# Attention and an MLP mixer in one kernel: two of six pairs of row tiles of the last batch's first channel product from seven half products, and a new order list

## The chip, the cores and the metric

The kernel runs on one core of one Trainium2 chip. A core has a matrix engine (TensorE, PE in the profile; its weight loads are PEld), three engines for element-wise work (VectorE, DVE; ScalarE, ACT; GpSimd, POOL), and an engine that mostly issues transfers (SyncE, SP). Each engine works through its own instructions in order and waits for others by semaphores. The metric is the device time of one execution in microseconds; the figure of a kernel is the median of its runs.

## The reference

Four batches, eight heads, 768 positions, 64 values a head. Attention sees a window of the last 128 positions and 4 sink positions. Its output, 768 x 512 for each batch, goes through a mixer: a product over positions, and then one over channels with 1536 hidden rows.

```
scores = (q @ k^T) / 8, kept where key < 4 or 0 <= query - key < 128
a = softmax(scores);  x = a @ v            # 768 x 512 for a batch
h = relu(x^T @ w_tok1) @ w_tok2            # over positions, 256 hidden
u = x + h^T
out = u + relu(u @ w_ch1) @ w_ch2          # over channels, 1536 hidden
```

Inputs and output are float32; the products are taken in bfloat16 and summed in float32.

## The kernel before

**Tiling.** Heads are handled in eight groups of four, g = 0 to 7, two groups to a batch. For a group, q and k are loaded, cast to bfloat16 (copies at L436 and L438) and turned; scores are formed at L827, the sink scores at L834, exponentials at L871, masks at L882 to L904 (on DVE or POOL, by the table MASK_ENG), and the weighted sums at L930 to L939. A weighted sum carries its row sum as a 65th column: DVE takes the reciprocal into one of four small tiles `rc` (L956, L963) and multiplies (L957, L969). The sink keys are copied to the tiles `ks` at L436 or L438 (engine by the table KS_ENG).

**Mixer.** The token products are at L1001 (with a ReLU into `h1` at L1060 or L1062) and L1043; L1049 adds to give `u`, and a DMA transpose (L1055) writes it as `uT`: four blocks of 128 channels by 768 positions. The first channel product makes tiles: one tile is 128 hidden rows by one half (384) of the positions, from four matmuls of 128x384 at L1103, and ACT or DVE writes its ReLU into `v1` (L1060, L1062). There are 12 row tiles and two halves, 24 tiles for a batch.

**Seven products, already there.** In the batches 1 to 3 the second channel product is cut into 2 x 2 blocks and formed by seven products of half size in place of eight. Its sums of `v1` are at L1129, its products at L1154, and the additions of its results on DVE at L1182 to L1187; stores are issued at L1240. The four sums of `w_ch2` that it needs are made once (L1078).

**What sets the order.** The program is a list of tasks, numbered as they are created (937 before). A planner in the file walks a simulated clock: whenever an engine is free, it takes the task that is ready and has the lowest number in the list RANK, one entry a task, and it hands a task with several possible engines to the one that would end it first. The order that comes out is the order in which instructions are issued; on the chip each engine keeps to it. PSUM is given out as eight banks: four singles (ps_ga to ps_gd) and two pairs (ps_sa, ps_sb); from a bank's first matmul to the last read of it no other task has it. Tasks that matter below: 340 and 341, a token product of batch 1 and its ReLU; 488, a cast of q for group 4; 23 and 24, the loads of the second half of `w_ch2` and of group 2's k, both on POOL's queue.

The core of a tile of the first channel product and the loop of the last three batches:

```
nc.tensor.matmul(flat(slot)[:, 0:HS], w_ch1[:, c, ts(ft, P)], uT_[:, c, ds(half * HS, HS)],
                 start=(c == 0), stop=(c == NC - 1))
...
for ft in range(NF):
    ch1(0, ft)
for x in range(NH):
    ch1(1, x)
    ch1(1, NH + x)
```

Of the kernel before, what the change touches and what calls it, by code (L numbers as in the profile page):

```python
# [46 lines left out]
MASK_ENG = {0: ('POOL',), 1: ('POOL', 'DVE'), 2: ('POOL',), 3: ('POOL',), 4: ('POOL', 'DVE'), 5: ('DVE',), 6: ('POOL',), 7: ('POOL',)}  # L47
KS_ENG = {0: ('ACT',), 1: ('POOL', 'ACT', 'DVE'), 2: ('POOL',), 3: ('ACT',), 4: ('POOL', 'ACT', 'DVE'), 5: ('ACT', 'DVE'), 6: ('ACT',
    'DVE'), 7: ('ACT', 'DVE')}
# [7 lines left out]
RANK = [-600, 12, 27, 429, 496, 90, 80, 0, 0, 10, 50, 100, 100, 140, 150, 1507, 62, 576, 219, 821, 901, 915, 1175, 1647, 1601, 2145,  # L57
    1923, 2170, 2665, 2875, 3140, 100, 90, 450, 210, 190, 1763, 1381, 1469, 1468, 1260, 1733, 3285, 3322, 95, 299, 389, 145, 379, 442,
    514, 731, 743, 0, 472, 507, 557, 803, 857, 894, 510, 655, 712, 836, 964, 1070, 1232, 1252, 708, 783, 574, 762, 873, 870, 1001, 1017,
    1152, 1164, 1282, 1299, 1479, 1410, 1547, 1640, 1584, 1529, 1604, 1677, 1701, 2119, 2114, 1916, 1972, 2086, 2166, 2132, 2156, 2111,  # L60
    2199, 2312, 981, 1053, 1235, 1303, -3, 1101, 1155, 1389, 1497, 1248, 1303, 1476, 1558, 1681, 1657, 1392, 1497, 1643, 1756, 1510,
    1407, 1712, 1787, 1772, 1907, 2076, 2226, 2127, 2185, 2249, 2279, 2157, 2229, 2895, 2249, 2265, 2388, 2390, 2456, 2480, 2038, 2671,
    2119, 1943, 2361, 2356, 2283, 2369, 1775, 2491, 2498, 2528, 2631, 3263, 3295, 3100, 3150, 2592, 2234, 2656, 3072, 3592, 3121, 3192,
    2924, 2994, 3023, 3093, 2895, 2795, 3170, 3241, 2974, 3424, 3220, 3290, 3789, 3875, 3724, 3810, 3404, 3550, 3334, 3420, 4179, 3745,
    3529, 3615, 3594, 3080, 3399, 3485, 3339, 3355, 4021, 4087, 3891, 4028, 4149, 4205, 4410, 5149, 4214, 4300, 3956, 4044, 4129, 4335,
    4475, 4578, 4570, 4626, 4727, 4946, 4822, 4909, 4662, 4782, 5010, 5118, 5263, 5369, 5348, 5434, 4857, 5055, 5480, 5569, 5964, 5709,
    5956, 6320, 6780, 6554, 6796, 6644, 6454, 6884, 6982, 6989, 7179, 7540, 7720, 7784, 7266, 7735, 7951, 8080, 8334, 8306, 8376, 8956,
    8785, 8850, 3951, 3767, 4045, 3745, 4116, 4144, 4377, 4433, 3857, 3942, 3854, 3912, 4054, 4013, 4314, 4368, 4518, 4605, 4713, 4819,
    5203, 5304, 5330, 5420, 4504, 5240, 5052, 5010, 5437, 5573, 5192, 5224, 5588, 5749, 5674, 5730, 5795, 5851, 5830, 5921, 5865, 6181,
    4850, 5107, 4808, 5770, 4977, 4911, 4963, 4998, 5413, 5480, 5446, 5521, 5586, 5606, 5612, 5695, 5936, 5900, 5989, 6058, 6164, 6205,  # L70
    6352, 6442, 5802, 5915, 6280, 6438, 6550, 6822, 6977, 7035, 6730, 6775, 6783, 6919, 7075, 7153, 7110, 7254, 7144, 7204, 6123, 6129,
    6108, 6265, 7417, 7504, 7352, 7438, 7648, 7734, 7834, 7542, 7794, 7959, 7821, 7908, 8084, 7864, 7967, 8209, 8071, 8142, 8384, 7907,
    8027, 8509, 4368, 4350, 4385, 4647, 4095, 4742, 4760, 4922, 8886, 8372, 8764, 8850, 8951, 9067, 9302, 9432, 9081, 9167, 8976, 9104,
    9277, 9323, 9447, 9469, 9432, 9518, 9926, 9972, 9725, 9811, 9660, 9746, 9790, 9876, 10527, 10613, 10272, 10358, 10267, 10213, 10402,
    10548, 10575, 10661, 10640, 10786, 10705, 10851, 10830, 10916, 11026, 11052, 11166, 11252, 11234, 11320, 10411, 10656, 10718, 10888,
    10840, 10935, 11079, 11220, 11305, 11404, 11485, 11580, 10397, 11119, 10895, 11393, 11487, 11628, 11648, 11654, 11713, 11314, 11472,
    11800, 11844, 11931, 12278, 11874, 10901, 11047, 11091, 11177, 11582, 11669, 12520, 11996, 12172, 12303, 12389, 12437, 11956, 12193,
    12240, 12511, 11305, 11422, 12041, 12127, 12299, 11865, 12237, 12324, 11975, 13099, 12565, 12633, 12371, 12496, 12561, 12707, 5274,
    5339, 5289, 5389, 5439, 6183, 6051, 5916, 6158, 6252, 6263, 6307, 6429, 6511, 6286, 6354, 6462, 6540, 6511, 7241, 6302, 6811, 6611,
    7483, 7561, 7630, 6898, 7067, 7133, 6988, 7000, 7085, 7646, 7573, 7737, 7377, 8059, 8092, 8353, 8402, 8114, 8162, 8184, 8252, 8149,  # L80
    8952, 8218, 8302, 5774, 5489, 5584, 5679, 5869, 6014, 6029, 6194, 7232, 6764, 6686, 7153, 7465, 6852, 7403, 8438, 8718, 8503, 8546,
    8636, 8829, 8907, 8976, 9226, 9246, 9193, 9363, 8653, 8703, 9019, 9107, 9380, 9449, 9075, 9258, 9497, 9542, 9521, 9592, 9556, 9492,
    9625, 9692, 9590, 9742, 8485, 8611, 8590, 8388, 9855, 9941, 9920, 10007, 10051, 10055, 10399, 10034, 10175, 10214, 10532, 10656,
    10684, 10137, 10175, 10619, 10180, 10234, 10809, 10224, 10294, 11329, 12901, 12957, 12564, 12692, 12629, 12715, 12694, 12790, 12816,
    12902, 13011, 13097, 12946, 13032, 13155, 13241, 13220, 13306, 13302, 13388, 13367, 13453, 13490, 13576, 13565, 13641, 13725, 13781,
    14120, 14086, 14065, 14151, 14160, 14246, 14335, 14421, 14583, 14679, 14979, 15065, 14452, 14547, 14914, 15000, 15164, 15250, 15262,
    15348, 14245, 14303, 14499, 14659, 15010, 15180, 15278, 15423, 15376, 15471, 15552, 14964, 14370, 14457, 14517, 14604, 15589, 15676,
    15524, 15592, 15741, 15958, 16045, 16092, 16024, 16152, 16343, 16293, 14648, 14724, 14725, 14817, 15890, 15936, 16176, 16305, 16307,
    16569, 16697, 16763, 16634, 16730, 16777, 16837, 14790, 15777, 15327, 15489, 16241, 16338, 16372, 16379, 16438, 16423, 16590, 16637,
    16700, 16973, 16887, 16711, 9134, 9249, 9324, 9514, 9609, 9799, 9854, 10024, 8397, 9826, 10144, 10623, 11001, 10994, 11219, 12376,  # L90
    12356, 12437, 12520, 12610, 12759, 12987, 12906, 13076, 13267, 12576, 13293, 12627, 12739, 12953, 13111, 13283, 13419, 13285, 13353,
    13432, 13477, 13456, 14127, 13620, 13676, 13655, 13726, 13690, 13776, 9989, 9894, 9419, 10524, 10119, 11064, 11444, 11569, 9641,
    10983, 11442, 12106, 12875, 11664, 12963, 13748, 13728, 13791, 13890, 13980, 13991, 14205, 14326, 14353, 14443, 14533, 13997, 14109,
    14341, 14547, 14707, 14843, 14713, 14767, 14856, 14910, 14880, 14960, 15044, 15100, 15079, 15178, 15119, 15446, 13955, 14021, 13879,
    13956, 15413, 15479, 15458, 15545, 15655, 15719, 15793, 15615, 15979, 16048, 15578, 15659, 15798, 15806, 15871, 16043, 16089, 16185,
    16433, 16132, 16245, 16518, 16765, 16851, 16895, 16981, 17871, 17957, 17155, 17241, 17025, 16811, 16830, 16916, 16960, 16986, 17030,
    17116, 17160, 17246, 17525, 17371, 17350, 17436, 18015, 17501, 17480, 17566, 18001, 18087, 17545, 17631, 17741, 17827, 17806, 17892,
    18262, 18348, 17936, 18022, 18197, 18283, 18327, 18413, 18392, 18478, 18522, 18608, 18457, 18543, 17685, 18141, 18221, 18302, 18076,
    18431, 18493, 18555, 18662, 18709, 18790, 18871, 18066, 18188, 17610, 18269, 18915, 19018, 18784, 18319, 19111, 18733, 18637, 19078,
    18926, 19132, 19180, 19272, 18132, 18350, 17676, 18397, 18980, 19067, 18849, 18952, 19177, 18718, 18838, 19413, 19439, 19526, 18973,  # L100
    19337, 18587, 18985, 19242, 19329, 19308, 19454, 19433, 19520, 19504, 19387, 19493, 20170, 19656, 19715, 17196, 19591, 19675, 19635,
    19690, 19765, 19669, 19723, 19757]
STRASSEN = {1, 2, 3}
EARLY_P = {1: 0, 2: 0, 3: 4}
TURNS = '10 20 11 21 60 50 61 40 70 51 41 30 12 71 22 62 52 31 72 32 42'
S_CHUNK = 2
S_ENG = {1: ('DVE',), 2: ('DVE',), 3: ('DVE',)}
T_ENG = ('POOL', 'DVE')

SEM = 0.05  # L110
PE_TAIL = 0.16


# [211 lines left out]
def dve(n):  # L325
    return n * 0.00104 + 0.065
# [11 lines left out]
def kernel(  # L338
# [13 lines left out]
    nc = tc.nc  # L352
# [436 lines left out]
    def make_scores(g):  # L789
# [84 lines left out]
        for j in range(2):  # L874
# [11 lines left out]
            def m1(t, dst=dst, lo=1, hi=NT):  # L886
# [11 lines left out]
                for i in range(2):  # L898
# [14 lines left out]
                    [G.exp[j, 1], G.exp[j, 2], t_mask1], prio=pr(g, "mk", j), port=True)  # L913
            G.ready[j, 0], G.ready[j, 1], G.ready[j, 2] = [a], [c], [d]

    rcs = [0]

    def make_pv(g):
        G, s, b = Gs[g], g % 2, g // GB
# [484 lines left out]
```

## Time and profile before

| | us |
|---|---|
| median of 10 runs | 200.41 (200.16 to 201.94) |
| profiled execution, its time | 201.38 |
| span of the profiled execution | 199.7 |
| PE busy | 193.3 |
| DVE busy | 135.4 |
| ACT busy | 108.7 |
| POOL busy | 77.0 |

The span runs from the first to the last instruction; 1.7 us of the execution lie around it. A row of the profile gives an engine, a line of the kernel, the operation, the tile written and the tiles read, and times in microseconds. A busy PE is not PE at its peak, since matmuls overlap their neighbours: how far apart neighbouring matmuls start says more. In a timeline, the brackets at the end of a row give the engine's idle time before it and what ended it.

### The profile page before, as it was taken

The page shows a single profiled execution, that of the slowest core. Times are in us where ns is not written, and L with a number is a line of the kernel's source. Part 1 is how long each engine was busy: PE and PEld are TensorE (multiplying, and loading weights), DVE is VectorE, ACT ScalarE, POOL GpSimd, SP SyncE. Part 2 cuts the span into 40 slices and gives each one's busy share as a digit, 9 for nine tenths or more (in the row PEclk, how much of TensorE's full clock was granted, in tenths as well). Part 3 has the DMA queues.
Part 4 walks back from the last instruction along what each step waited for, and adds up shares of the span by engine and source line. Part 5 has one row for each costly group of instructions (what it writes and reads, how often), then busy time and mean ns, then how long its engine had stood idle before and what let it go on. Part 6 is the DMA issues. An engine that isn't in the chain of part 4 may idle for free.

```text
span 199.7 us, 4626 instructions
## 1 busy us (share of the span) xinstructions
PE 193.3 (97%) x1799; PEld 130.0 (65%) x1799; DVE 135.4 (68%) x312; ACT 108.7 (54%) x191; POOL 77.0 (39%) x132
## 2 busy tenths in 40 slices
PE   7999999999998999999999999999999999999993
PEld 2544876656675565666756687567677787666882
DVE  4688872479758489757578865475799974146883
ACT  2799478889897833289425202867824003764100
POOL 8994432125999663200632020992970000000000
PEclk9999999999999999999999999999999999999999
DMA  5999999999399999899997998350000168000053
GB/s 171 363 225 181 208 279 271 225 268 192 101 281 181 249 169 129 226 127 240 214 171 131 185 196 184 113 128 0 0 3 0 32 171 257 21 0 0 0 187 132
DMA packets 75016, 31.00 MB, mean 155 GB/s; under 512 B 63667, under 2 KB 71475, under 8 KB 74995
## 3 DMA queue, kind: packets, MB, share of 16 engines
q0 software_dynamic: 29680, 10.22, 41.9%
q1 hardware_dynamic: 44082, 18.85, 41.6%
q10 hardware_dynamic: 1232, 1.64, 2.3%
q8 instruction: 14, 0.23, 0.5%
q14 instruction: 8, 0.06, 0.1%
HBM read 26.77 MB, written 6.29 MB: 166 GB/s over the span
## 4 chain that ended last, share of the span: by engine, by line
PE 74%; DMA 15%; DVE 4%; SPq 2%; POOL 2%; issue 1%; ACT 0%; ACTq 0%; DVEq 0%; POOLq 0%
DMA w_tok<-in_moe_w_tok_dram 8%; PE ps_gd L1103 8%; PE ps_ga L1103 7%; PE ps_gb L1103 7%; PE ps_gc L1103 7%; PE ps_gd L1154 5%; PE ps_gc L1154 4%; PE ps_gb L1154 4%; DMA q32b<-in_q_dram 4%; DMA k32a<-in_k_dram 3%; PE ps_ga L1154 3%; SPq L481 2%; PE ps_sa L1154 2%; PE ps_sa L827 2%; PE ps_ga L1262 1%; PE ps_gd L1262 1%
## 5 line engine op out<-in xcount | busy, mean ns | idle before, releaser
L1103 PEld LDWEIGHTS <-w_ch 128*128 128x128 bf16 x384 | 36.5, 98 | 22.9 <-issue 0.8
L1154 PEld LDWEIGHTS <-v 128*128 128x128 bf16 x222 | 21.0, 98 | 4.3 <-issue 0.9
L1060 ACT ACTIVATE v<-ps_ga 128x384 bf16<-128x384 f32 x22 | 10.8, 491 | 15.9 <-PE ps_ga L1103 14.9
L1060 ACT ACTIVATE v<-ps_gb 128x384 bf16<-128x384 f32 x20 | 9.8, 492 | 11.5 <-PE ps_gb L1103 11.0
L1060 ACT ACTIVATE v<-ps_gd 128x384 bf16<-128x384 f32 x15 | 7.4, 491 | 9.3 <-PE ps_gd L1103 9.2
L1103 PE MATMUL ps_gb<-uTb,w_ch 128*128 128x384 bf16 x56 | 11.4, 326 | 0.0
L481 POOL DMA_DIRECT2D vab<-in_v_dram x4 | 5.7, 1437 | 14.0 <-PE ps_gd L939 11.4
L1060 ACT ACTIVATE v<-ps_gc 128x384 bf16<-128x384 f32 x18 | 8.8, 491 | 4.0 <-PE ps_gc L1103 3.6
L1103 PE MATMUL ps_gd<-uTa,w_ch 128*128 128x384 bf16 x52 | 10.6, 326 | 0.0
L1262 PEld LDWEIGHTS <-v 128*128 128x128 bf16 x72 | 6.3, 98 | 6.3 <-issue 1.0
L1001 PEld LDWEIGHTS <-w_tok 128*128 128x128 bf16 x96 | 9.1, 98 | 1.9 <-issue 0.4
L1103 PE MATMUL ps_gc<-uTa,w_ch 128*128 128x384 bf16 x48 | 9.8, 326 | 0.0
L1103 PE MATMUL ps_ga<-uTa,w_ch 128*128 128x384 bf16 x48 | 9.8, 326 | 0.0
L1103 PE MATMUL ps_gc<-uTb,w_ch 128*128 128x384 bf16 x44 | 9.0, 326 | 0.0
L1103 PE MATMUL ps_ga<-uTb,w_ch 128*128 128x384 bf16 x44 | 8.9, 326 | 0.0
L481 POOL DMA_DIRECT2D vaa<-in_v_dram x4 | 5.9, 1478 | 7.3 <-PE ps_gb L939 6.0
L1129 DVE TENSOR_TENSOR x_bb<-v 128x768 bf16<-128x768 bf16 x6 | 3.7, 615 | 7.2 <-ACT v L1060 7.2
L1103 PE MATMUL ps_gd<-uTb,w_ch 128*128 128x384 bf16 x40 | 8.1, 326 | 0.0
L882 POOL TENSOR_TENSOR pTa<-pTa,mask 128x512 bf16<-128x512 bf16 x2 | 2.3, 1153 | 13.7 <-ACT pTa L871 13.7
L871 ACT ACTIVATE pTc<-ps_sb 128x1024 bf16<-128x1024 f32 (+1 forms) x6 | 5.8, 959 | 3.3 <-PE ps_sb L827 3.3
L1103 PE MATMUL ps_gb<-uTa,w_ch 128*128 128x384 bf16 x36 | 7.3, 326 | 0.0
L871 ACT ACTIVATE pTb<-ps_sa 128x1024 bf16<-128x1024 f32 (+1 forms) x7 | 7.0, 997 | 0.5 <-PE ps_sa L827 0.5
(429 smaller groups left out, 555.0 us busy)
## 6 DMA issues: line engine op xcount, KB each, us to landing
q32a<-in_q_dram SPq DMA_DIRECT2D x4, 384.0 KB, 5.5
vaa<-in_v_dram POOLq DMA_DIRECT2D x4, 384.0 KB, 11.2
vab<-in_v_dram POOLq DMA_DIRECT2D x4, 384.0 KB, 12.0
w_ch<-in_moe_w_ch_dram POOLq DMA_DIRECT2D x3, 512.0 KB, 14.9
w_ch<-in_moe_w_ch_dram POOLq DMA_DIRECT2D x2, 768.0 KB, 20.1
q32b<-in_q_dram SPq DMA_DIRECT2D x8, 192.0 KB, 4.5
k32b<-in_k_dram SPq DMA_DIRECT2D x8, 192.0 KB, 6.5
out_dram<-oa SPq DMA_DIRECT2D x4, 256.0 KB, 6.6
```

The source lines that it names most:

```text
L481: t = add(eng, hold, lambda t: e.dma_start(out=o, in_=i), deps, prio=prio, dma=work, run=run)
L827: nc.tensor.matmul(half(slot, i)[:, at:at + w].rearrange("p (c q) -> p c q", q=P), qkT(kT, g, j)[ds(64 * i, 64), kt], qkT(qT, g, j)[ds(64 ...
L871: nc.scalar.activation(dst[:, :, 512 * u:512 * u + w], ps_s[slot.at[1]][:, :, 0:w], AF.Exp, scale=scale)
L882: on(t).tensor_tensor(out=dst[:, :, 0:2 * P], in0=dst[:, :, 0:2 * P], in1=mask0.rearrange("p i c q -> p i (c q)"), op=ALU.mult)
L1001: nc.tensor.matmul(flat(slot)[:, 0:GH * D], w_tok1[:, n, ts(tt, P)], x[:, n, ds(a * GH * D, GH * D)], start=(n == 0), stop=(n == NT - 1))
L1060: nc.scalar.activation(o, i, AF.Relu)
L1103: nc.tensor.matmul(flat(slot)[:, 0:HS], w_ch1[:, c, ts(ft, P)], uT_[:, c, ds(half * HS, HS)], start=(c == 0), stop=(c == NC - 1))
L1129: on(t).tensor_tensor(out=sums_a[n][:, r], in0=in0, in1=in1, op=op)
L1154: nc.tensor.matmul(flat(slot)[:, 0:cw], A[n][0][:, x, ts(i, P)], W[n][:, x, ds(c0, cw)], start=(first and x == 0), stop=(x == NH - 1), ski ...
L1262: nc.tensor.matmul(flat(slot)[:, 0:cw], v1[:, ft, ts(st, P)], w_ch2[:, ft, ds(c0, cw)], start=(ft == 0), stop=(ft == NF - 1 and (b > 0 or ...
```

## The change

Only the last batch's first channel product is rewritten; the order list is replaced as a whole.

- Row tile i and row tile 6 + i form a pair, for both halves of the positions: four tiles. With HALF_PAIRS = 2 the pairs 0 and 1 are no longer formed from 4 x 4 matmuls but from seven products of two matmuls each, in the form of Strassen and Winograd: on 2 x 2 blocks of `w_ch1` (channels by rows) and of `uT` (channels by positions). The other 16 tiles stay as they were. The order in which the tasks are created is TILES: a tile is its half and its row tile in hexadecimal, p0 and p1 are the pairs.
- For them, four sums of blocks of `w_ch1` (128x512 bfloat16, on POOL or DVE) are written over the old q and k buffers `qb` and `kb`, and four sums of blocks of `uT` (128x768, on DVE) over the old `va`.
- In a pair the results are put together by one copy on ACT, five additions on DVE, one ReLU from PSUM and three ReLUs from SBUF on ACT or POOL.
- The masks of group 5 go from DVE to POOL; the `ks` copies of group 0 may go to any of three engines.
- The plan now holds a task that writes a reciprocal tile until the last reader of that tile has been placed.
- RANK has 963 entries in place of 937.

```diff
-MASK_ENG = {..., 5: ('DVE',), ...}
-KS_ENG = {0: ('ACT',), ...}
+MASK_ENG = {..., 5: ('POOL',), ...}
+KS_ENG = {0: ('POOL', 'ACT', 'DVE'), ...}
...
-RANK = [-600, 12, 27, 429, 496, 90, 80, ...]
+RANK = [-500, 24, 27, 449, 556, 90, 80, ...]
...
+HALF_PAIRS = 2
+TILES = '05 0b 04 0a 03 p0 09 02 08 p1 15 1b 14 1a 13 19 12 18'
...
+    rc_use = [None] * 4
...
+            last_rc = rc_use[rcs[0] % 4:rcs[0] % 4 + 1]
...
-                m = add("DVE", 0.1, er, [m], prio=pr(g, "no"))
+                m = add("DVE", 0.1, er, [m, last_rc], prio=pr(g, "no"))
...
+                rc_use[slot_rc] = G.norm[-1]
...
+        def pairs_of_tiles():
...
+            t_w = chain(Sw, (*w, [(0, a21, a22, ALU.add, 0), (1, Sw[0], a11, ALU.subtract, 0), (2, a11, a21, ALU.subtract, 0),
+                                  (3, a12, Sw[1], ALU.subtract, 0)]), [*l_ch1, *late], T_ENG, 60,
...
+            t_u = chain(Tu, (*x_, [(0, b12, b11, ALU.subtract, 0), (1, b22, Tu[0], ALU.subtract, 0), (2, b22, b12, ALU.subtract, 0),
+                                   (3, b21, Tu[1], ALU.subtract, 0)]), [*M.turn, *Gs[NG - 2].pv, *Gs[NG - 1].pv], "DVE", 5,
...
+                def product(k, slot, first, stop, deps=()):
+                    def f(t):
+                        for c in range(NC // 2):
+                            nc.tensor.matmul(flat(slot)[:, 0:HS], L[k](c), R[k][:, c], start=(first and c == 0), stop=(c == NC // 2 - 1),
+                                             skip_group_check=True)
...
+                p1 = product(1, a, True, True)
+                e0 = add("ACT", act(HS), lambda t: nc.scalar.activation(t0, flat(a)[:, 0:HS], AF.Copy), [p1, *before, *t_temp], prio=5.1, slot=a)
+                p6 = product(6, bb, True, True)
+                r2 = plus(t2, bb, t0, [p6, e0, *before])
+                p5 = product(5, c_, True, True)
+                p2 = product(2, a, False, True, [e0])
+                put(0, f_lo, None, p2, a)
+                p7 = product(7, bb, False, True, [r2])
+                r3 = plus(t3, bb, t0, [p7, r2])
+                r22 = plus(t3, c_, t3, [p5, r3])
+                put(1, f_hi, t3, r22)
+                p4 = product(4, bb, False, True, [r3])
+                p3 = product(3, c_, False, True, [r22])
+                r21 = plus(t0, bb, t0, [p4, r3], True)
+                put(0, f_hi, t0, r21)
+                r12 = plus(t2, c_, t2, [p3, r2, r22], True)
+                put(1, f_lo, t2, r12)
...
+        elif b == B - 1 and b in STRASSEN and HALF_PAIRS:
+            one = pairs_of_tiles()
+            for n, x in enumerate(TILES.split()):
+                if n == len(TILES.split()) - 4:
+                    M.early_prio = next(seq)
+                if x[0] == "p":
+                    one(int(x[1]))
+                else:
+                    ch1(int(x[0]), int(x[1], 16))
+            products()
```

In a pair, P1 to P7 below are the calls product(1) to product(7); `plus` is an addition on DVE that reads PSUM and an SBUF tile of 128x384 float32, `put` a ReLU into `v1`.

## The prediction

> **What bounds the kernel now.** I read the page's first two parts, the stretches of the last 63 us, the chain of waits, and the order of time around the one long wait of TensorE.
>
> ```profile
> PE 193.3 (97%) x1799; PEld 130.0 (65%) x1799; DVE 135.4 (68%) x312; ACT 108.7 (54%) x191; POOL 77.0 (39%) x132
> PEclk9999999999999999999999999999999999999999
> ```
>
> TensorE (PE) is the bound, and the throttle takes nothing. The stretches (span, then busy us of PE, PEld, DVE, ACT, POOL, then clock and DMA) show how tight it is:
>
> ```profile
> 137.50:150.00 12.50, 12.38 (x125) 8.81 (x122) 9.68 (x21) 7.80 (x15) 9.85 (x18) 1.00 0.00 1
> 150.00:163.00 13.00, 13.00 (x120) 9.99 (x117) 12.28 (x28) 2.14 (x5) 0.00 (x0) 1.00 0.20 42
> 166.77:184.99 18.22, 18.22 (x123) 11.74 (x121) 7.05 (x16) 11.01 (x23) 0.00 (x0) 1.00 0.16 58
> ```
>
> The last row is the stage that the change rewrites, the first channel product of the last batch. PE never idles there, while VectorE (DVE) has 11 us free and GpSimd (POOL) everything. So work taken off PE comes off the end one for one, if what replaces it keeps up. The two rows above are the other side: DVE has 12.50 - 9.68 = 2.8 us free in the first and 0.7 us in the second.
>
> In the chain, in order of time, one tile of this stage follows the next at its own length:
>
> ```profile
> 166.93 0.65 PE ps_ga L1103 x4
> 167.58 0.65 PE ps_gc L1103 x4
> ```
>
> The waits of PE hold one that is neither start-up nor structure, and the order of time says why:
>
> ```profile
> PE ps_gc L834 <- DVE h1b L1062: 0.7, 1, 0.7
> ...
> 58.37 0.82 PE L1001 MATMUL ps_gc<-x_bb,w_tok 128*128 128x256 bf16 x6
> 59.82 1.16 DVE L438 CAST qba<-q32a 128x768 bf16<-128x768 f32 x1 [1.69 <-DMA q32a<-in_q_dram]
> 60.90 0.41 DVE L1062 TENSOR_SCALAR h1b<-ps_gc 128x256 bf16<-128x256 f32 x1
> 61.37 0.29 PE L834 MATMUL ps_gc<-qTb,ksb 128*32 128x256 bf16 x4 [0.70 <-DVE h1b L1062]
> ```
>
> The product in bank ps_gc was done at 59.19. Its ReLU stood on DVE behind a cast that idled 1.69 us for a DMA and then took 1.16 us beside POOL's masks, and PE waited 0.70 us for the bank.
>
> **The change, part by part.**
>
> *The seven products.* A tile costs four 128x384 matmuls, 0.65 us, so 0.1625 us each. Two pairs were 8 tiles, 32 matmuls; they become 2 x 7 products of two, 28. Four fewer: **-0.65 us**. The Trainium skill, "TensorE: Matmul & The Clock Gate", section "Back-to-back issue gap", speaks against this size: it says that in a stream of load and matmul the spacing is about 81 ns at 128 columns and 131 ns at 512, so the isolated formula over-counts. By it, my straight line at 384 columns gives 114 ns, and the saving is an estimated 0.46 us. The trace has 0.65 for four, tile after tile; I take the row.
>
> *Do the pairs make PE wait?* The order list sets, on PE: tiles 05 0b 04 0a 03 09, then (a prime for the second pair) P1 P5, tile 02, P6 P2, tile 08, P1' P7 P6' P5' P2' P4, tile 15, P3, and P4', P7', P3' between tiles of the second half. P2 needs ACT's copy of P1: 0.325 (P1) + 0.20 (PE to ACT, from 166.77 + 0.65 to 167.62) + 0.49 (L1060) + 0.1 = 1.1 us after P1 starts; before P2 stand P1, P5, tile 02, P6 = 1.6 us. P7 waits for a DVE addition after P6. Its price: 0.42 us for 256 and 0.69 for 512 columns give 0.55 for 384; P6 ends at 1.6, + 0.2 + 0.55 + 0.1 = 2.5, and P7 stands at 1.6 + 0.325 (P2) + 0.65 + 0.325 = 2.9. P4 waits for the addition after P7: 2.9 + 0.3 + 0.2 + 0.65 = 4.1, and stands at 2.9 + 4 x 0.325 = 4.2. Every cover holds, the last by 0.1 us: **0**; without these covers about 0.5 us a pair, 1.0 us at most.
>
> *DVE in this stage.* Four differences of uT, 128x768 bf16, at 0.56 (L1129 here): 2.2 us; five additions a pair, 10 x 0.55 = 5.5 us. 7.05 + 7.7 = 14.8 of 17.6 us: it holds. They start when the last transpose has landed, 167.28 by its issue at 164.84 and 2.4 us of flight, and take about 2 us; P5 stands at 166.77 + 6 x 0.65 + 0.33 = 171.0. Covered. ACT loses 8 evictions of 0.49 and gains 2 copies, 2 evictions and up to 6 ReLUs from SBUF of about 0.5 (it or POOL): 11.0 - 3.9 + 5.0 = 12.1 of 17.6 us. **0**. The buffers are old ones, and no DMA is added.
>
> *Four differences of w_ch1.* 128x512 bf16 each, on DVE or POOL, possible once the last attention groups are transposed. The list puts them near 138 to 143, beside POOL's masks of the last group (9.85 us of POOL in the first stretch). The row for 128x512 on DVE is 0.42 alone and 0.61 beside POOL (L882), POOL's own is 1.16. Here the second rule decides: the Trainium skill, "SBUF — State Buffer", section "Who interferes with whom", says that a DVE instruction with two SBUF inputs and a POOL instruction that reads SBUF exclude each other for a whole instruction. The trace agrees in the same stretch: the 128x768 difference takes 0.55 alone, but 1.33 at 143.86. By the row alone the four cost 4 x 0.42 = 1.7 us and vanish in 2.8 us of free DVE; by the lock up to 4 x (0.42 + 0.78) = 4.8 us, 2.0 more than is free, and behind them on DVE are the last group's normalizations, the sums and the evictions that PE's products need. Bounds 0 and 2.0; by the nearer row (4 x 0.61 = 2.4, which fits, but in pieces) I take **+0.25**.
>
> *Masks of group 5 on POOL.* DVE loses 4.3 us of masking (two of 0.42, then 0.76, 1.03, 1.71) between 85.7 and 94.7. A half takes POOL 4.9 us (138.71 to 143.62). The last exponential ends at 93.39; POOL, two operations behind, would end near 95.7 instead of 94.67. Late by a microsecond are the last three weighted sums, and the vab load queued behind the masks on POOL (96.56 now, waiting for them). PE has tiles at L1103 from 96.00 on to fill with: **0**, if they are not used up before; else 1.0.
>
> *ks copies of group 0 on any engine.* 0.43 us may leave ACT at 12.66, where ACT is 98% busy. But PE is next held by the w_tok load, which lands at 26.64, so **0**; bounds -0.4 and 0.1.
>
> *Order.* The second half of w_ch2 is now issued before group 2's K on POOL's queue, both behind w_tok. It can share bandwidth with w_tok, whose landing released PE after a gap of 0.25 us: between -0.25 and, if w_tok is slowed by one issue (0.8 us), +0.8; I take 0. At the 0.70 us wait, the list now ranks the ReLU (5969) just ahead of the cast (5971), where it had the cast first (6158 to 6265), and lifts the product that feeds it. If the ReLU is issued first, it runs at 59.3 and the wait is gone: **-0.70**; bounds 0 and -0.86, the whole gap. What is late next is nothing there: the cast waits for its DMA until 59.8 anyway.
>
> *Waits on the reciprocal tiles.* They order the list only; no instruction is added. DVE's reciprocals already follow the reads four uses before them. **0**.
>
> **Sum:** -0.65 + 0.25 - 0.70 = -1.10 us. The profiled execution has a span of 199.7 and a time of 201.38, so 1.7 us lie around the span, which nothing here touches. 198.6 + 1.7 = 200.3 for that execution. It is one of the longer ones: the median is 200.41, so the median becomes 199.3.
>
> **The rivals.** *Arithmetic alone:* the ReLU still stands behind the cast, because the cast is ready first in the order as written, and -0.65 + 0.25 gives 200.0; without the 0.25, 199.8. For it: the two ranks are only 2 apart. Against: the product is lifted, and there are other gaps of 0.3 (71.3, 114.1, 145.3) that a new order may close.
>
> *The lock wins, slower:* DVE and POOL block each other between 137 and 150, the last group's mask chain and DVE's sums are late, and the next stretch cannot absorb it, with 0.7 us free on DVE. Price 2.0 from above, and the 0.70 of the wait not won: 200.41 - 0.65 + 2.0 = 201.8. It cancels the saving from 0.65 us of new PE idle time in 137 to 163, and shows as slower from 1.65. For it: PE already has gaps of 0.16 and 0.29 there. Against: the differences are needed only at 171 and can wait for a free moment.
>
> **How the numbers follow.** A measurement of this kernel can tell about 0.5%, 1.0 us: 199.41 and 201.41 are the bounds. Forecast 0.50 (0.44 of it below 199.41; own range 198.4 to 199.8); arithmetic alone 0.28 (0.04 below); lock 0.22 (0.18 above 201.41). Faster 0.48, same 0.34, slower 0.18. The range runs from 198.4 (-0.65, the whole 0.86, and 0.5 of the other gaps) to 201.5, just inside the slower case.
>
> **What would show it.** Right: 28 matmuls of the new line where 32 of L1103 stood, back to back at 0.1625 us; the stage from its first tile to the last 0.65 us shorter; no wait at L834 near 60; PE idle in 137 to 163 not above 0.4 us. Wrong: PE gaps ahead of P4 or P7 (covers too thin), DVE's differences of w_ch1 at 1 us and more with POOL's masks stretched beside them (lock), the first tile of the last batch later than 166.8 (either), or a PE gap near 26 (load order).

## The result and the profile after

The changed kernel takes 199.12 us (median of 14 runs, 198.95 to 200.47) against 200.67 for the kernel before (49 runs, 200.16 to 204.64). The ratio is 0.9919, with a 95% interval of 0.9897 to 0.9941. The profiled execution of the changed kernel has a time of 199.24 and a span of 197.5.

The lines of the page of the changed kernel that answer to those shown of the kernel before are these.

```profile
PE 192.1 (97%) x1795; PEld 129.6 (66%) x1795; DVE 138.2 (70%) x321; ACT 107.3 (54%) x189; POOL 86.4 (44%) x151
PEclk9999999999999999999999999999999999999999
```

TensorE has four instructions fewer and is still the bound. DVE and POOL have more to do, ACT less. The same stretches as in the prediction (span, then busy us of PE, PEld, DVE, ACT, POOL, then clock and DMA), in the changed kernel:

```profile
137.50:150.00 12.50, 12.47 (x131) 9.07 (x129) 10.64 (x26) 7.67 (x14) 10.32 (x18) 1.00 0.01 1
150.00:163.00 13.00, 13.00 (x112) 10.25 (x111) 11.57 (x28) 1.26 (x3) 0.00 (x0) 1.00 0.28 64
166.77:184.99 18.22, 18.22 (x128) 12.32 (x127) 13.29 (x30) 10.95 (x24) 1.87 (x2) 1.00 0.12 43
```

PE still never idles in the last row, and DVE, at 13.29 us, is not full. In the first row PE is busier than before (12.38), although DVE and POOL both do more beside each other. (The bounds are those of the prediction; the changed kernel is 0.8 to 1.4 us ahead of that profile here, so its rows hold slightly later work.)

In the chain, part of the rewritten stage looks like this; L1174 is the line of the pairs' products:

```profile
169.45 0.33 PE ps_gd L1174 x2
169.78 0.33 PE ps_gb L1174 x2
170.10 0.65 PE ps_gc L1111 x4
170.75 0.33 PE ps_ga L1174 x2
```

The waits of PE in the changed kernel (what it waited for; us in total, times, longest):

```profile
PE ps_ga L1473 <- DVE warm L445: 1.2, 1, 1.2
PE ps_sb L813 <- ACT pTc L874: 0.4, 1, 0.4
PE ps_sa L817 <- ACT pTa L874: 0.2, 1, 0.2
```

The wait of 0.70 us at the sink scores is not in this list. That looks as forecast, but the order of time around it, shown with the experiments, does not bear the reason out.

At a granted clock of 1.0 both kernels have executions that are about 1 us longer than their other ones. The profiles of the kernel before at 201.38 and 201.45 (run b0_again) are of this kind; the one at 200.36 (run b0_third) is called ordinary here. The ratios, and the medians of the experiments, leave out slow runs (all but one at a granted clock of 0.85 to 0.992), among them the profiled execution of b1_relu_first. Gaps of PE are worked out below from the starts of its matmuls, less the spacing that the trace shows for their columns (162.5 ns for 384, 109 for 256, 56 for 128).

**Where the time went.** Ordinary execution against ordinary execution, cut at the same matmuls. The changed kernel's lines stand 8 lower at the start of the mixer's code and 104 at its second half, so L1154 is L1258 there.

| stretch, by the start of its first matmul | before (b0_third) | after | difference |
|---|---|---|---|
| start, to batch 1's second token product | 74.65 | 74.83 | +0.18 |
| to the first second channel product | 27.73 | 27.75 | +0.02 |
| to the last token product | 57.26 | 56.70 | -0.56 |
| to the last 128x384 matmul (the stage rewritten) | 24.17 | 23.52 | -0.65 |
| to the last matmul | 11.20 | 11.25 | +0.05 |

The sum is -0.96 us. The two executions' own times differ by 1.12; the rest lies behind the last matmul. The first row is within the scatter: other runs with the changed kernel's order in this stretch reach the same product at 74.54 (a2_masks_dve) and 74.66 (a1_no_pairs). So the gain has two parts, 0.65 from the pairs' products and 0.56 from a stretch in which these products do not run at all.

### The profile page after: what moved, and what is told of

Its sections match the earlier page's. It is cut to its first block, busy times and chain, and to the rows that moved or that the text cites. A ratio compares the mean times of both kernels' runs of the same rounds, so it can differ in the third digit from the quotient of the medians.

```text
span 197.5 us, 4652 instructions
## 1 busy us (share of the span) xinstructions
PE 192.1 (97%) x1795; PEld 129.6 (66%) x1795; DVE 138.2 (70%) x321; ACT 107.3 (54%) x189; POOL 86.4 (44%) x151
## 4 chain that ended last, share of the span: by engine, by line
PE 93%; ACT 3%; DVE 1%; issue 1%; DVEq 0%
PE ps_gd L1111 8%; PE ps_gb L1111 8%; PE ps_ga L1111 7%; PE ps_gd L1258 6%; PE ps_gb L1258 5%; PE ps_gc L1111 5%; PE ps_gc L1258 4%; PE ps_ga L1258 3%; PE ps_sa L830 3%; PE ps_gd L1366 3%; PE ps_gb L1366 3%; PE ps_ga L1473 2%; PE ps_sa L1258 2%; PE ps_sb L830 2%; PE ps_gd L1009 2%; PE ps_ga L1009 2%
## 5 line engine op out<-in xcount | busy, mean ns | idle before, releaser
L1111 PEld LDWEIGHTS <-w_ch 128*128 128x128 bf16 x352 | 33.3, 98 | 20.5 <-issue 0.6
L1258 PEld LDWEIGHTS <-v 128*128 128x128 bf16 x222 | 21.2, 98 | 4.2 <-issue 0.2
L1068 ACT ACTIVATE v<-ps_gc 128x384 bf16<-128x384 f32 x13 | 6.4, 490 | 16.2 <-PE ps_gc L1111 15.5
L1111 PE MATMUL ps_gd<-uTa,w_ch 128*128 128x384 bf16 x72 | 14.7, 326 | 0.0
L1068 ACT ACTIVATE v<-ps_ga 128x384 bf16<-128x384 f32 x16 | 7.9, 491 | 5.4 <-PE ps_ga L1111 5.3
L1111 PE MATMUL ps_gb<-uTa,w_ch 128*128 128x384 bf16 x52 | 10.6, 326 | 0.0
L874 ACT ACTIVATE pTc<-ps_sb 128x768 bf16<-128x768 f32 (+1 forms) x6 | 5.5, 921 | 3.6 <-PE ps_sb L830 3.6
L441 POOL CAST qbb<-q32b 128x768 bf16<-128x768 f32 x5 | 4.1, 830 | 7.3 <-DMA q32b<-in_q_dram 7.3
L441 POOL CAST kbb<-k32b 128x768 bf16<-128x768 f32 x5 | 4.3, 851 | 5.5 <-DMA k32b<-in_k_dram 5.5
L830 PEld LDWEIGHTS <-kTa 64*128 64x128 bf16 x96 | 3.5, 94 | 4.8 <-issue 3.8
L904 POOL TENSOR_SCALAR_AFFINE_SELECT pTc<-pTc 128x256 bf16<-128x256 bf16 (+1 forms) x12 | 6.2, 520 | 0.9 <-ACT pTc L874 0.9
```

The costliest lines, as they stand in the source:

```text
L441: on(t).tensor_copy(out=o, in_=i)
L830: nc.tensor.matmul(half(slot, i)[:, at:at + w].rearrange("p (c q) -> p c q", q=P), qkT(kT, g, j)[ds(64 * i, 64), kt], qkT(qT, g, j)[ds(64 ...
L874: nc.scalar.activation(dst[:, :, 512 * u:512 * u + w], ps_s[slot.at[1]][:, :, 0:w], AF.Exp, scale=scale)
L904: nc.gpsimd.affine_select(out=cur, in_=cur, compare_op=ALU.is_ge, fill=0.0, base=0, pattern=[[0, hi - lo], [1, P]], channel_multiplier=-1)
L1068: nc.scalar.activation(o, i, AF.Relu)
L1258: nc.tensor.matmul(flat(slot)[:, 0:cw], A[n][0][:, x, ts(i, P)], W[n][:, x, ds(c0, cw)], start=(first and x == 0), stop=(x == NH - 1), ski ...
```

## The experiments

Labels in b start from the kernel before, labels in a from the changed one. Durations of stretches are those of a run's profiled execution.

**Two more looks at the kernel before** (b0_again, b0_third: no edit). The question is whether the gap of 0.70 us belongs to the kernel.

> The kernel before, unchanged, to see whether its one long gap on TensorE near 60 us repeats. If it is made by the order of the instructions: the gap of 0.86 us ahead of the sink products at L834 is there again, within 0.2 us. If it was a chance of that one execution (a transfer that landed late, a collision with GpSimd): gone or under 0.3 us.

> The kernel before once more, for a profile of one of its ordinary executions (its time near 200.4; both profiles so far were of longer ones, 201.4). If the gap near 60 us belongs to the longer executions: time near 200.4, gap at L834 under 0.2 us, first token product of batch 1's second kind at 74.6 in place of 75.6 us. If it is in every execution: 0.3 us or more.

b0_again took 201.45 us, again a longer execution. It has a gap of 0.48 us at L834, by the starts, where the first profile has 0.86: less than was expected of a gap that the order makes, more than of a chance. The cast of q starts late again (59.69) but takes 0.77 us in place of 1.16; two more gaps, of 0.33 and 0.51 us, follow at 63.17 and 64.03, where PE waits for DVE's work on k. b0_third took 200.36, and had no gap at L834. The order of time on b0_third:

```profile
58.93 1.13 DVE L438 CAST qba<-q32a 128x768 bf16<-128x768 f32 x1 [0.72 <-DMA q32a<-in_q_dram]
59.99 0.41 DVE L1062 TENSOR_SCALAR h1b<-ps_gc 128x256 bf16<-128x256 f32 x1
...
60.67 0.29 PE L834 MATMUL ps_gc<-qTb,ksb 128*32 128x256 bf16 x4
```

The cast still stands ahead of the ReLU, and it still waits for the load of q. But the load has landed 0.9 us earlier (the cast starts at 58.93, not at 59.82), and the ReLU is done at 60.40, before PE asks for the bank. No order had to change for the gap to vanish.

**The ReLU ahead of the cast, alone** (b1_relu_first).

```diff
 todo = plan.order()
+x = plan.tasks[341]            # the ReLU at L1062
+todo.remove(x)
+todo.insert(todo.index(plan.tasks[488]), x)   # the cast at L438
```

> The kernel before with one instruction moved: on VectorE the ReLU of h1b goes ahead of the cast of q that it stood behind near 60 us. Theory of the prediction (the ReLU behind the cast makes TensorE wait for a bank, and TensorE is the bound): the wait at L834 is gone and the time falls by 0.7 to 0.9 us, to 0.996 of before. Rival (a gap won there is given back at the next wait, for a transfer or a transpose): TensorE is ahead by 0.8 us at 62 us and no longer at 75 or at the end; ratio 1.000.

Measured: 200.35 us, ratio 1.0001 (0.997 to 1.0031). Two places on DVE's queue are all that differs, and nothing is won; whether the move would shorten a longer execution is not shown. And in the changed kernel the ReLU was not moved:

```profile
58.63 0.82 PE L1009 MATMUL ps_gb<-x_bb,w_tok 128*128 128x256 bf16 x6
59.48 0.78 DVE L441 CAST qba<-q32a 128x768 bf16<-128x768 f32 x1 [1.09 <-DMA q32a<-in_q_dram]
60.19 0.40 DVE L1070 TENSOR_SCALAR h1b<-ps_gb 128x256 bf16<-128x256 f32 x1
60.85 0.29 PE L837 MATMUL ps_gb<-qTb,ksb 128*32 128x256 bf16 x4
```

The cast starts at 59.48 and the ReLU follows it, although its rank is the lower one. Where the load is late in this order as well, in the profiled execution of a5 (below), the cast starts at 60.35 and PE has a gap of 0.51 us at L837. Whether PE waits there depends, in both kernels, on when that load lands and on how long the cast then takes.

**The pairs alone, and everything but the pairs** (b2_pairs, a1_no_pairs; a0_again is the unchanged kernel beside them). b2 is the kernel before with the two pairs, its ranks up to there untouched:

```diff
-RANK = [ranks of the changed kernel]
+RANK = [the 822 first ranks of the kernel before, then the changed kernel's, + 100 for the differences of w_ch1, + 45 for the rest]
-MASK_ENG = {..., 5: ('POOL',), ...}
+MASK_ENG = {..., 5: ('DVE',), ...}
-KS_ENG = {0: ('POOL', 'ACT', 'DVE'), ...}
+KS_ENG = {0: ('ACT',), ...}
...
-[m, last_rc]
+[m]
-[m, *old, last_rc]
+[m, *old]
```

> The kernel before with the two pairs from seven products alone; the order of everything ahead of 142 us is that of before. Theory (four matmuls fewer): the stage from its first tile to the last of its 128x384 products is 0.65 us shorter, and the time falls by 0.65 us, to 0.997, less what the four differences of w_ch1 cost beside GpSimd's masks (0 to 0.25). Rival (the lock between VectorE and GpSimd decides): the last batch's first tile starts 0.7 to 2 us later than in before, the time is the same or longer, 1.000 to 1.007.

a1 is the changed kernel with its order and engines, but eight ordinary tiles in place of the pairs and no sums (RANK loses the entries of the sums, and has those of the eight tiles in place of the pairs'):

```diff
-one = pairs_of_tiles()
+def one(i):
+    for half, ft in ((0, i), (0, NH + i), (1, i), (1, NH + i)):
+        ch1(half, ft)
```

> The changed kernel with the two pairs formed as eight ordinary tiles again, and the eight sums left out; all other work in the changed kernel's order. Theory (the pairs give their four matmuls and nothing else, and the rest of the gain is the order list's): the stretch from the last token product to the last 128x384 matmul is 24.2 us in place of 23.5, and the time is 0.65 us above the changed kernel, 0.996 of before. Rival (most of the gain is the pairs'): 0.999 to 1.000. The stretch from 103 us to the last token product, 57.3 in before, 57.6 with the pairs alone, 56.7 in the changed kernel: if the four differences of w_ch1 cost 0.3 there whatever the order, it falls to 56.4 here; if the new order hides them, it stays at 56.7.

> The changed kernel once more on the same chip as the others, to compare them with it: 0.992 of before, its last matmul starting within 0.3 us of 194.05 us.

| run | median us | ratio, 95% interval | first second channel product to last token product | stage of the pairs |
|---|---|---|---|---|
| before (b0_third) | | 1 | 57.26 | 24.17 |
| b2_pairs | 200.28 | 0.9993 (0.9969 to 1.0016) | 57.60 | 23.51 |
| a1_no_pairs | 200.36 | 0.999 (0.9967 to 1.0013) | 57.16 | 24.26 |
| a0_again | 199.24 | 0.9929 (0.991 to 0.9948) | 56.69 | 23.52 |

The last column is clear: 0.66 and 0.74 us for the pairs' products, whatever the order. But b2 pays 0.34 back in the stretch before, and a1 has only 0.10 of the 0.56 there, although its ranks are the changed kernel's. Neither half alone can be told from the kernel before. Two places on DVE's queue explain most of the differences between these runs.

The first is between 140 and 146 us. The order of time of b0_third, DVE's in one fence and PE's in the next:

```profile
141.87 0.56 DVE L1062 TENSOR_SCALAR v<-ps_gc 128x384 bf16<-128x384 f32 x1 [0.34 <-PE ps_gc L1103]
...
142.87 1.31 DVE L1129 TENSOR_TENSOR k32a<-q32a,v 128x768 bf16<-128x768 bf16 x1
144.10 0.54 DVE L1062 TENSOR_SCALAR v<-ps_gc 128x384 bf16<-128x384 f32 x1
```

```profile
142.48 0.81 PE L1103 MATMUL ps_gc<-uTa,w_ch 128*128 128x384 bf16 x4
...
143.79 0.81 PE L1103 MATMUL ps_gb<-uTa,w_ch 128*128 128x384 bf16 x4
144.70 0.81 PE L1154 MATMUL ps_gc<-w_ch,v 128*128 128x256 bf16 x6
```

Both times PE waits for bank ps_gc. The tile at 142.48 comes 0.16 us late, when the ReLU at 141.87 has read the bank. Then L1154 writes the bank that the ReLU at 144.10 reads. That ReLU stands on DVE behind a difference of 1.31 us, beside POOL's masks; the same difference takes 0.55 where POOL is quiet. PE comes 0.26 us late (144.70, where 143.79 + 0.65 = 144.44 was possible). In the changed kernel, DVE and then PE:

```profile
141.45 0.62 DVE L1143 TENSOR_TENSOR kbb<-w_ch,qbb 128x512 bf16<-128x512 bf16 x1
141.99 0.87 DVE L1233 TENSOR_TENSOR k32a<-q32a,v 128x768 bf16<-128x768 bf16 x1
142.78 0.55 DVE L1070 TENSOR_SCALAR v<-ps_gd 128x384 bf16<-128x384 f32 x1
143.58 0.54 DVE L1070 TENSOR_SCALAR v<-ps_ga 128x384 bf16<-128x384 f32 x1
```

```profile
142.31 0.81 PE L1111 MATMUL ps_ga<-uTa,w_ch 128*128 128x384 bf16 x4
...
143.62 0.81 PE L1111 MATMUL ps_gd<-uTa,w_ch 128*128 128x384 bf16 x4
144.26 0.82 PE L1258 MATMUL ps_ga<-w_ch,v 128*128 128x256 bf16 x6
```

The difference stands 0.9 us earlier, is over in 0.87, and both ReLUs follow it; the tile at 142.31 has another bank, and PE's matmuls follow each other without a gap. In a1, where the planner has no sums of `w_ch1` to place, four tasks of DVE stand as in the kernel before, and the difference is long again:

```profile
142.69 1.31 DVE L1234 TENSOR_TENSOR k32a<-q32a,v 128x768 bf16<-128x768 bf16 x1
```

PE's gaps are back too, 0.16 at 142.30 and 0.27 at 144.52; they are nearly all of what a1 lacks. Both gaps stand in the profiles without the pairs (before, b0_again, b0_third, a1), and neither in those with the fourth difference of `w_ch1` on DVE (after, a0_again, b2, b3), under either list; a4, with all four on POOL, has the first alone. So these 0.42 us come with the pairs, through the place of their differences on DVE's queue, though not from their products. No run moved one of these ReLUs alone.

The second is the last group's last normalization, which a token product waits for. b2 has the good order at the first place too, its differences of `w_ch1` at the same times as the changed kernel (136.38 to 141.43). But its DVE, in order of time:

```profile
151.70 0.55 DVE L1235 TENSOR_TENSOR v<-v,k32a 128x768 bf16<-128x768 bf16 x1
152.17 0.17 DVE L964 RECIPROCAL rcd<-ps_gc 128x4 f32<-128x4 f32 x1
152.38 0.42 DVE L965 TENSOR_TENSOR x_bb<-ps_gc,rcd 128x256 bf16<-128x256 f32 x1
```

Three sums of v1 stand ahead of the normalization, which starts at 152.38. In the changed kernel it starts at 150.98, ahead of them, and in b0_third at 151.02. In b2 PE idles 0.41 us for it, and 0.15 more at the next product. Here the new list is what helps.

Over this whole stretch the gaps of PE from 0.14 us upward are 0.30, 0.16, 0.26, 0.16 and 0.14 in b0_third, 1.02 us in all; in the changed kernel 0.17, 0.19 and 0.16, 0.52 in all. These 0.50 are nearly all of the 0.56: 0.42 at the first place, and 0.13 ahead of a product at 113.5 that waits for a sum of `v1` in both (0.30 and 0.17). The 0.13 is the new list's, for b2 has 0.30 there.

The same stretch (102.40 to 159.60 us) of b0_third, b2 and the changed kernel, span, then PE, PEld, DVE, ACT, POOL:

```profile
102.40:159.60 57.20, 56.91 (x519) 41.03 (x519) 42.91 (x98) 25.29 (x48) 22.86 (x41) 1.00 0.45 96
```

```profile
102.40:159.60 57.20, 56.73 (x518) 41.01 (x518) 43.34 (x102) 25.27 (x47) 21.98 (x39) 1.00 0.47 91
```

```profile
102.40:159.60 57.20, 57.16 (x524) 41.44 (x522) 44.35 (x103) 25.51 (x48) 21.40 (x39) 1.00 0.54 92
```

PE is busy 56.91, 56.73 and 57.16 of 57.20 us. The changed kernel has the most on DVE and the least idle time on PE: the order decides, not DVE's load.

**The new order from 107 us on, the old one ahead of it** (b3_late_order).

```diff
-RANK = [ranks of the changed kernel]
+RANK = [the entry of the kernel before for each task that it starts ahead of 100 us, the changed kernel's + 100 for the others]
```

Engines, and the waits on the reciprocal tiles, are as in b2.

> The kernel before with the pairs and the changed kernel's order list for what comes after 100 us alone; ahead of 107 us order, engines and loads are those of before (masks of group 5 on VectorE, ks of group 0 on ScalarE). Theory (in ordinary executions the whole gain is the pairs' 0.65 us and gaps of TensorE closed by the order between 103 and 160 us, 0.6 us): as fast as the changed kernel within 0.3 us, 0.992 to 0.994 of before, the stretch from 103 us to the last token product at 56.7 us. Rival (the early order, the masks on GpSimd or the loads carry a part): 0.995 to 0.998, with that stretch at 56.7 and the loss ahead of 103 us.

Measured: 200.02 us, ratio 0.9951 (0.9919 to 0.9982). That is 0.9 us above the changed kernel, and where the rival had it, with the loss ahead of 103 us. (The runs of the kernel before that stand beside b3, a5 and a6 have more of the longer executions, a mean of 201.14 against 200.63 to 200.69 beside the others, so these three ratios are about 0.0025 lower than the others would make them.) Its two stretches are 56.69 and 23.52, those of the changed kernel. But its profiled execution is 0.88 us late at batch 1's second token product (75.71 against 74.83), and not because of the wait at the sink scores:

```profile
59.80 0.56 DVE L443 CAST qba<-q32a 128x768 bf16<-128x768 f32 x1 [1.44 <-DMA q32a<-in_q_dram]
...
67.47 0.83 POOL L443 CAST qbb<-q32b 128x768 bf16<-128x768 f32 x1 [1.83 <-DMA q32b<-in_q_dram]
...
70.05 0.20 PE L941 MATMUL ps_ga<-vab,pTd 128*128 128x65 bf16 x1 [0.56 <-POOL pTd L906]
```

The cast of q starts as late as in the first profile (59.82) but takes 0.56 us, and PE does not wait for it. PE waits at 70.05, 0.72 us by the starts, for a mask that stands on POOL behind the cast of another tile of q, whose load landed late (the cast starts at 65.82 in b0_third). The lowest run of b3, 199.19, is the changed kernel's ordinary time. So by the stretches the order after 107 us and the pairs carry the gain of an ordinary execution. The longer ones may depend on what was changed ahead of that: 17 of 49 runs of the kernel before are at 201.15 us or more, 2 of 14 of the changed kernel at 200.4, and only 4 of 12 of b3 below 199.6. Whether that is the early order or chance, and what makes the loads of q land late, was not found.

**The differences of `w_ch1` on POOL** (a4_sums_pool): the rival that ends slower, with the differences forced onto the engine of the masks.

```diff
-..., [*l_ch1, *late], T_ENG, 60,
+..., [*l_ch1, *late], ("POOL",), 60,
```

> The changed kernel with the four differences of w_ch1 on GpSimd alone, where the plan puts them ahead of the last group's masks. The theory of the slower rival (that group's masks are on the path that ends at the last batch's first tile): four times 1.16 us of mask delay, of which 1 to 2 us come out as gaps on TensorE between 140 and 166 us; time 0.997 to 1.002 of before. The other theory (TensorE has tiles of batch 2 to fill with): within 0.4 us of the changed kernel, 0.992 to 0.994.

Measured: 200.47 us, ratio 1.0 (0.9971 to 1.0029). The stretch from 102 to the last token product takes 58.01, 1.31 more than in the changed kernel. POOL's order of time in a4:

```profile
134.41 1.16 POOL L1143 TENSOR_TENSOR qba<-w_ch 128x512 bf16<-128x512 bf16 x1
135.64 1.16 POOL L1143 TENSOR_TENSOR qbb<-qba,w_ch 128x512 bf16<-128x512 bf16 x1
136.75 1.16 POOL L1143 TENSOR_TENSOR kba<-w_ch 128x512 bf16<-128x512 bf16 x1
138.57 1.16 POOL L885 TENSOR_TENSOR pTc<-pTc,mask 128x512 bf16<-128x512 bf16 x1 [0.66 <-ACT pTc L872]
```

Against the changed kernel, where DVE does three of the four ahead of the masks:

```profile
136.39 0.42 DVE L1143 TENSOR_TENSOR qba<-w_ch 128x512 bf16<-128x512 bf16 x1
136.90 0.43 DVE L1143 TENSOR_TENSOR qbb<-qba,w_ch 128x512 bf16<-128x512 bf16 x1
137.24 0.42 DVE L1143 TENSOR_TENSOR kba<-w_ch 128x512 bf16<-128x512 bf16 x1
```

In the changed kernel POOL's first mask starts at 137.71, so three differences run at the price of DVE alone, and only the fourth, at 141.45, is lengthened (0.62). On POOL each takes 1.16. (This execution of a4 is a longer one: it was already 0.87 us behind at batch 1's second token product, 75.70 against 74.83, so its times are to be read less 0.87, and its first mask is not late.) The two gaps of PE that a4 adds, 1.02 behind the matmul at 152.46 and 0.26 behind that at 154.71, make up its 1.31; the longest wait of PE in this stretch is for a normalization of the last group:

```profile
PE ps_sb L1258 <- DVE x_bb L963: 0.9, 1, 0.9
```

The last normalization starts at 154.60 here, 2.75 us later than in the changed kernel, less the 0.87. Part of it comes from the masks: the fourth difference stands among them on POOL (1.15 at 141.47), and their last one ends at 149.19, against 148.03, 0.29 later. The larger part seems to be the order, which the planner changed with the engine: three differences of v1, at 151.42 to 152.91, and others stand ahead of the normalizations. So the slower rival's end is real, a late last group that costs enough to cancel the whole gain; that DVE and POOL lock each other is not what brought it about here.

**The pairs without their covers** (a6_bare_pairs): the ordinary tiles between a pair's products must now wait for the end of the pair.

```diff
+after_pair = []
...
-m = add("PE", pe(*[HS] * NC), f, [*M.turn[...], ...
+m = add("PE", pe(*[HS] * NC), f, [*after_pair, *M.turn[...], ...
...
-p1 = product(1, a, True, True)
+p1 = product(1, a, True, True, after_pair)     # p6 and p5 too
...
+after_pair[:] = [p3, p4]
```

> The changed kernel with each pair's seven products run without ordinary tiles between them. The prediction put this at 0.5 us a pair, 1.0 in all. Worked out again from the rows: P2 at 1.1 us after P1, P6 to 1.75, P7 at 2.6, P4 at 3.8, P3 to 4.7 us in place of 2.3 us of products: 2.4 us a pair, so 4 to 5 us in all with TensorE idle between 169 and 180 us; time 1.012 to 1.018 of before.

Measured: 202.22 us, ratio 1.0054 (1.0024 to 1.0085), 3.0 us above the unchanged a0_again, where 4 to 5 were expected. Three of its products in pair 0, with the idle time of PE ahead of them:

```profile
169.75 0.48 PE L1175 MATMUL ps_ga<-uTb,w_ch 128*128 128x384 bf16 x2 [0.31 <-ACT q32b L1200]
...
171.27 0.48 PE L1175 MATMUL ps_gb<-vab,kba 128*128 128x384 bf16 x2 [0.72 <-DVE q32b L1182]
172.41 0.48 PE L1175 MATMUL ps_gb<-vab,w_ch 128*128 128x384 bf16 x2 [0.65 <-DVE q32b L1182]
```

P2 waits for ACT's copy, P7 and P4 for DVE's additions. By the starts pair 0 loses 2.43 us (0.47 + 0.88 + 0.81 + 0.27) and pair 1 only 0.42, as products of the second channel product fill in there. A pair that has only itself to run loses 2.4 us, as was expected before this run, not the prediction's 0.5.

**Masks of group 5 back on DVE, the loads in the old order, no waits on the reciprocal tiles** (a2_masks_dve, a3_loads_old, a5_no_rc_waits): the three edits costed at nothing, each undone alone.

```diff
+for n in range(555, 561):      # a2: masks of group 5
+    plan.tasks[n].on = "DVE"
```

```diff
+x = plan.tasks[24]             # a3: group 2's K ahead of the half of w_ch2, on POOL's queue
+todo.remove(x)
+todo.insert(todo.index(plan.tasks[23]), x)
```

```diff
-[m, last_rc]                   # a5
+[m]
-[m, *old, last_rc]
+[m, *old]
```

> The changed kernel with the masks of group 5 on VectorE again, every instruction at its place in the order. Theory (the move is hidden behind tiles): same as the changed kernel within 0.2 us, 0.992 to 0.993 of before. Rival (the move frees VectorE for something that TensorE waits for): 0.3 to 1.0 us longer, visible as gaps on TensorE between 85 and 103 us.

> The changed kernel with group 2's k issued ahead of the second half of w_ch2 again on GpSimd's queue. Theory (the earlier weight load takes transfer time from w_tok, which landed 0.26 us later in the changed kernel and releases TensorE near 27 us): w_tok lands at 26.6 in place of 26.9 and the time falls by 0.2 to 0.3 us, 0.991 of before. Rival (the gain is given back at later transfers): the same within 0.1 us.

> The changed kernel planned without the waits between uses of the reciprocal tiles; the order of 9 instructions moves, around 23 and 85 us. Theory (they order the list only and cost nothing): the same as the changed kernel within 0.2 us, 0.992 to 0.993 of before. Rival (they keep a reciprocal from standing on VectorE behind ScalarE's read): gaps on TensorE near 23 us of 0.2 us and more, 0.994 or above.

| run | median us | ratio, 95% interval |
|---|---|---|
| a2_masks_dve | 200.14 | 0.9992 (0.9971 to 1.0012) |
| a3_loads_old | 199.05 | 0.9917 (0.9886 to 0.9947) |
| a5_no_rc_waits | 199.31 | 0.992 (0.9892 to 0.9948) |

Loads and waits are worth nothing that can be told. a2 loses the gain: it is 0.9 us above a0_again. Its stretch with group 5 takes 28.47 us against 27.75, and PE has gaps of 0.14, 0.39 and 0.19 between 93.4 and 96.3; the rest of the 0.9 was not traced. This does not show that the move to POOL brings time: the kernel before, with the masks on DVE in an order of its own, has 27.73 there. It shows that the new order relies on POOL.

## Why the prediction was right, and where it was not

- **Seven products, -0.65: right, by the row.** The stage is 0.65 us shorter (24.17 to 23.52), and 0.66 and 0.74 in b2 and a1, which change the pairs and what the planner moves with them. The estimate of 0.46 from the Trainium skill's page "TensorE: Matmul & The Clock Gate", section "Back-to-back issue gap", does not hold for 384 columns here; the chain after has the pairs of such matmuls at 0.33 us and each four at 0.65, as before. The measurement decides.
- **The pairs' covers, 0: right. Their price, "about 0.5 us a pair, 1.0 us at most": wrong.** Bare pairs cost 3.0 us. The prediction gives no working for the 0.5, which is about one such wait; in a pair four products wait one after another (P2, P7, P4, P3), 0.27 to 0.88 us each.
- **DVE and ACT in the stage, 0: right.** From its first tile at 165.39 the stage takes 17.57 us; DVE was busy 12.60 of them (14.8 of 17.6 was forecast), ACT 10.89 (12.1). PE idled nowhere. The ReLU that went to POOL took 1.18 us where about 0.5 was taken for it, and that delayed nothing.
- **Four differences of `w_ch1`, +0.25 between 0 and 2.0.** In the changed kernel no cost is to be seen. The prediction had all four beside POOL's masks; three of them start at 136.39 to 137.24 and end ahead of the first mask, where the lock that the Trainium skill's page "SBUF — State Buffer", section "Who interferes with whom", describes has nothing to hold, and the fourth, at 141.45, is lengthened by 0.2. The 0.34 of b2 has the size that was taken, but not the cause: its differences run as in the changed kernel, and a late normalization costs 0.41 and 0.15. On POOL, in the order that follows from it, 1.31 (a4). As a cost the bounds hold, and where in the order the differences stand decides between them; counted with the 0.42 us of gaps that are gone where the fourth stands on DVE, the sign was wrong.
- **Masks on POOL, 0: right** for the order made for it. POOL ended with group 5 at 94.88 (94.47 + 0.41), which is the forecast 95.7 less the 0.8 us by which that profile is later here (103.37 against 102.58 at the first second channel product), and the stretch took 27.75 against 27.73.
- **Copies, loads, reciprocal tiles, 0: right**; the bounds of -0.25 and 0.8 for the loads were not needed, and a3 and a5 show no effect of the loads and the waits. The copies were never undone alone.
- **The 0.70 us at the sink scores: the step that failed.** It said that the ReLU, ranked just ahead of the cast, would run before it at 59.3. It does not; the cast still goes first (59.48 before 60.19), as the first rival had it: a rank only decides among tasks that are ready. Nor was there a gap to win in an ordinary execution: it comes with the late load of some longer ones, and b1 shows that to move the ReLU alone brings nothing that can be told. The prediction knew that its profile was "one of the longer ones", and still took the gap off the median. So it is luck that the sum comes out. What stands in this term's place is another, -0.56 us, nearly all from small gaps between 103 and 160, which the prediction had only in its rival's line as "other gaps of 0.3 ... that a new order may close".
- **The sum.** Ordinary against ordinary, -0.65 and -0.56, the scatter of +0.18 and 0.07 in the other two rows make the -0.96, where -1.10 was forecast. The medians differ by 1.55, since the kernel before has more of the longer executions; the prediction has no term for that. The forecast of 199.3 against 199.12 is therefore closer than its terms deserve.
- **The signs named beforehand**: 28 matmuls of the new line, no gap in the stage, PE's gaps in 137 to 163 of 0.35 us (0.19 + 0.16, under 0.4), the first tile of the last batch at 165.39 (before 166.77, in the ordinary b0_third 165.75). All held. "No wait at L834" held too, and is a sign that could not tell the cause.

## What to carry to other kernels

Before a gap in a profile is explained or priced, compare the profiled execution's own time with the median: a gap of a longer execution is not there to win in the others. A fast product with fewer matmuls pays off one for one when TensorE is full, but only if tiles that need nothing lie between its products: here the cover is worth 3.0 us and the saving 0.65. When DVE works beside POOL's masks, look not at the lengthened operation but at what is queued behind it: one ReLU that frees a bank, put after a difference of 1.31 us, cost PE 0.26 us, while four further differences on DVE (0.42, 0.43, 0.42 and 0.62 us) cost it nothing that can be seen, and the last of them even goes with an order in which that wait is gone.

## What the hardware showed that was not expected

- At a granted clock of 1.0 some executions of one kernel take about 1 us longer than others. The time is lost in the first 76 us, and not always at one place: PE idles 0.86 us at 61.37 in the first profile of the kernel before, 0.48 there and 0.33 and 0.51 soon after in b0_again, 0.72 at 70.05 in b3, 0.74 at 15.65 in a4. From there on the stretches of the kernel before agree within 0.02 us in all three of its profiles (27.73, then 57.26 to 57.28, 24.17 and 11.20). The cause is open.
- The same cast of 128x768 on DVE took 1.13, 1.16, 0.78, 0.60 and 0.56 us in five executions, and the same difference of 128x768 took 0.55, 0.87 and 1.31, the long ones beside POOL's masks.
- On POOL a ReLU of 128x384 float32 into bfloat16 took 1.18 us, a cast of 128x256 0.69 us.
